# Zeros at the start of a linear-attention and MoE kernel: forty-four products in 64 by 64 tiles, and planned waits near the beginning filled with half the columns

## The chip, the cores and the metric

The kernel runs on one core of one Trainium2 chip. The metric is the time of one execution on the device, in microseconds. Before the change three timed runs gave 536.9, 537.01 and 539.99 us, a median of 537.01 us. One further execution was recorded by the hardware profiler. It took 540.65 us, and 538.9 us lie between its first and its last instruction (the span).

## The reference

A linear attention with a decay for each channel runs over four batches, eight heads and 768 tokens, with heads 48 wide. Its output, 3072 tokens of 384 numbers, goes through two matrix products with a gate between them. All numbers are float32.

```python
for t in range(S):
    kt, vt, rt, wt = (k[:, :, t], v[:, :, t], r[:, :, t], w[:, :, t])
    cur = np.einsum('bhd,bhe->bhde', u[None] * kt, vt)
    y[:, :, t] = np.einsum('bhd,bhde->bhe', rt, state + cur)
    state = wt[:, :, :, None] * state + np.einsum('bhd,bhe->bhde', kt, vt)
...
h = x @ w_in                       # 384 -> 2048
g = np.where(pos, h, np.where(neg, 0.0, (h + beta) ** 2 / (4.0 * beta)))
return (g @ w_out).astype(np.float32)
```

## The kernel before, in words

The tokens are cut into twelve units of 256 (`attention(u, ...)`) and into six blocks of 512 for the two big products (`products(n)`). For each unit the decays `wq` are turned into running products by scans on VectorE (lines 472 and 477), `k` and `r` are scaled with them (498 and 548), and TensorE makes the products among the tokens of a chunk (`among`, line 518), the transposes of `k` (`ktrans`, 557), the state updates (`umat`, 579) and the outputs (627). `among` runs twice for the first three units, the first time on `nk`, which is `k` times `u` from ScalarE (line 488). These attention products are 64 by 64 tiles of float32 in turn on the four quarters of the array; the transposes take 128 by 128.

The sixteen blocks of weights come as raw words (`wraw`, loaded at line 386) and are decoded: ScalarE (398 and 400), GpSimd (402), VectorE (404), ScalarE (394) and VectorE (407). The big products are lines 974 (into `h`) and 994 (into `acc`). `load` (line 333) issues nearly all transfers from SyncE's queue.

The order of all this is not written by hand. `Plan` holds each piece of work as an operation with an engine, an assumed cost, what it reads and writes, and a due time; `best` and `order` make a list for each engine from these. Three things in it concern TensorE alone and compute nothing:

- `warm()` runs `WARM` = 44 products of a tile of zeros (`zero`, set by GpSimd at line 338) with itself, before anything else has to run there. The planner assumes a cost of 5.0 us for them. Each takes the whole array (128 by 128 weights) and 32 columns, through the helper `zeros` (line 357).
- `kept_warm` walks the planned order, and where TensorE is planned to be idle for longer than `IDLE` = 0.6 us, it puts more zeros into a bank that is free at that time, as many columns as fit the gap at `COLUMN` = 0.00168 us each. These are the fills; they too are line 357.
- The gap from time zero to the first operation of TensorE counts as a wait as well: `free` starts at 0.0, and so a fill stands even ahead of the 44 products.

Since all of it is float32, the trace shows two records for one such product, and two weight loads.

TensorE takes its instructions in this fixed order. A zero product that takes longer than planned holds up what is behind it, whether its data are there or not.

Of the kernel before, what the change touches and what calls it, by code (L numbers as in the profile page):

```python
# [42 lines left out]
WARM = 44  # L43

IDLE, COLUMN = 0.6, 0.00168

LANES = 8

# [6 lines left out]
class Plan:  # L55
# [97 lines left out]
    def kept_warm(self, order, engine, banks, fill):  # L153

        ops, begin, end = self.ops, self.begin, self.end
        touched, free, out = {}, 0.0, []
        used = {b: [n for n in order if b in ops[n]["touch"]] for b in banks}
        for n in order:
            op = ops[n]
            if op["e"] == engine:  # L160
                gap = begin[n] - free
                if gap > IDLE:
                    for b in banks:
                        after = next((m for m in used[b] if begin[m] >= begin[n]), None)
                        before = max((end[m] for m in used[b] if begin[m] < begin[n]), default=0.0)
                        if (after is None or ops[after]["fresh"]) and begin[n] - max(before, free) > 0.9 * gap:
                            out.append(lambda b=b, gap=gap: fill(b, gap))
                            break
                free = begin[n] + op["cost"]
            out.append(op["emit"])  # L170
        return out
# [102 lines left out]
def attention_moe(tc, a):  # L274
    nc = tc.nc
    V, A, G, PE = nc.vector, nc.scalar, nc.gpsimd, nc.tensor
# [7 lines left out]
    def tiles(n, shape, dt, name, of=pool):  # L284
        return [of.tile(shape, dt, tag=f"{name}{i}", name=f"{name}{i}") for i in range(n)]

    def one(shape, dt, name, of=pool):
        return tiles(1, shape, dt, name, of)[0]
# [10 lines left out]
    zero = one([128, 128], F32, "zero")  # L299
# [22 lines left out]
    hp = tiles(2, [128, WIDE], F32, "h", psum)  # L322

    bank = [*tiles(3, [128, 512], F32, "bank", psum), *acc, *hp]

    def op(engine, cost, due, reads, writes, emit, **kw):
        return plan.add(engine, cost, emit, due, reads, writes, **kw)
# [8 lines left out]
    SOON = 0, 200.0  # L336
# [15 lines left out]
    def zeros(to, n):  # L352

        while n >= 32:
            m = min(512, n if n < 128 else n // 128 * 128)
            rhs = zero[:, 0:m] if m <= 128 else zero.unsqueeze(1).broadcast_to([128, m // 128, 128])
            PE.matmul(to[:, 0:m], lhsT=zero, rhs=rhs, start=True, stop=True)  # L357
            n -= m

    def warm():  # L360
        for _ in range(WARM):
            zeros(hp[0], 32)

    op("PE", 5.0, SOON, ["zero"], [("b", 6)], warm)


    wraw, w_hi, w_lo = {}, {}, {}
# [472 lines left out]
    for n in range(2 * GUARDED):  # L840
# [10 lines left out]
        out=flag, in0=bank[0][0:1, 0:1], scalar1=127.5, scalar2=None, op0=ALU.is_lt))  # L851

    with tc.manual_schedule(engines=None):
        for emit in plan.kept_warm(plan.best(step_ops, dues), "PE", [("b", i) for i in range(8)],
                                   lambda b, us: zeros(bank[b[1]], int((us - 0.25) / COLUMN))):
            emit()

    for p in (psum, pool):
# [204 lines left out]
```

## Time and profile before

| what | value |
|---|---|
| timed runs, median (lowest to highest) | 537.01 us (536.9 to 539.99) |
| profiled execution | 540.65 us |
| its span | 538.9 us |
| TensorE busy | 524.8 us, 97% |
| VectorE busy | 339.4 us, 63% |
| ScalarE busy | 299.1 us, 56% |
| GpSimd busy | 92.3 us, 17% |
| granted clock, mean | 0.995 |
| moved by DMA | 55.03 MB, mean 102 GB/s |

Time is counted in microseconds from the start of the span. In the rows of the trace the first number is a start, the second a duration; then come engine, line and operation, the tile written, an arrow and the tiles read, and the shapes. In brackets stands how long the engine had been idle, and what ended that. `x88` says that so many records are merged in a row. PE is TensorE's products, PEld its weight loads, DVE is VectorE, ACT ScalarE, POOL GpSimd, and SPq the queue of SyncE that issues transfers. The zeros of the fills and of `warm` count as busy time of TensorE.

### The profile page before, as it was taken

The page shows a single profiled execution, that of the slowest core. Times are in us where ns is not written, and L with a number is a line of the kernel's source. Part 1 is how long each engine was busy: PE and PEld are TensorE (multiplying, and loading weights), DVE is VectorE, ACT ScalarE, POOL GpSimd, SP SyncE. Part 2 cuts the span into 40 slices and gives each one's busy share as a digit, 9 for nine tenths or more (in the row PEclk, how much of TensorE's full clock was granted, in tenths as well). Part 3 has the DMA queues.
Part 4 walks back from the last instruction along what each step waited for, and adds up shares of the span by engine and source line. Part 5 has one row for each costly group of instructions (what it writes and reads, how often), then busy time and mean ns, then how long its engine had stood idle before and what let it go on. Part 6 is the DMA issues. An engine that isn't in the chain of part 4 may idle for free.

```text
span 538.9 us, 13106 instructions
## 1 busy us (share of the span) xinstructions
PE 524.8 (97%) x5556; PEld 438.4 (81%) x5556; DVE 339.4 (63%) x596; ACT 299.1 (56%) x617; POOL 92.3 (17%) x63
## 2 busy tenths in 40 slices
PE   8999989999999999999999999999999999999993
PEld 6977878787899999887878787778877787888882
DVE  5079979998888687744778643887353444333330
ACT  2058869897986556544456354556444434544440
POOL 2053466663120202000102101110000100000000
PEclk9999999999999999999999999999999999999998
DMA  8609481634661515310424301430100100100001
GB/s 323 264 16 338 151 293 77 232 112 137 198 229 52 177 27 202 98 60 2 134 96 137 138 1 48 156 118 6 60 1 0 55 3 13 63 0 0 1 0 66
DMA packets 22067, 55.03 MB, mean 102 GB/s; under 512 B 3120, under 2 KB 8688, under 8 KB 22000
## 3 DMA queue, kind: packets, MB, share of 16 engines
q1 hardware_dynamic: 21856, 53.98, 29.1%
q8 instruction: 45, 0.74, 0.6%
q14 instruction: 22, 0.18, 0.1%
q10 hardware_dynamic: 144, 0.13, 0.1%
HBM read 47.22 MB, written 4.72 MB: 96 GB/s over the span
## 4 chain that ended last, share of the span: by engine, by line
PE 92%; DVE 2%; ACT 1%; SPq 1%; DMA 1%; issue 1%; POOL 0%; DVEq 0%; POOLq 0%
PE h L974 37%; PE acc L994 37%; PE bank L627 4%; PE h L357 3%; PE bank L357 3%; PE bank L579 2%; PE bank L518 2%; PE bank L557 2%; SPq L726 1%; DMA x<-last 1%; DVE fl L404 1%; PE acc L518 0%; DVE r L524 0%; ACT g L789 0%; PE acc L702 0%
## 5 line engine op out<-in xcount | busy, mean ns | idle before, releaser
L974 PE MATMUL h<-x,wt 128*128 128x512 f32 (+1 forms) x1035 | 222.9, 361 | 2.4 <-DMA x<-last 2.1
L974 PEld LDWEIGHTS h<-x,wt 128*128 128x128 f32 x1035 | 170.7, 188 | 33.7 <-DMA x<-last 2.1
L994 PE MATMUL acc<-gh,wt 128*128 128x512 f32 (+1 forms) x690 | 156.4, 362 | 0.0
L791 DVE SCALAR_TENSOR_TENSOR g<-g,h 128x512 f32<-128x512 f32 (+1 forms) x115 | 68.1, 593 | 108.3 <-ACT g L790 106.2
L994 PEld LDWEIGHTS acc<-gh,wt 128*128 128x128 f32 x690 | 115.6, 188 | 21.3
L789 ACT ACTIVATE g<-h 128x512 f32<-128x512 f32 (+1 forms) x115 | 60.6, 527 | 124.1 <-PE h L974 117.2
L794 DVE TENSOR_TENSOR gl<-g,gh 128x512 fp32r<-128x512 f32 (+1 forms) x115 | 71.3, 624 | 28.1 <-ACT gh L793 27.7
L994 PE MATMUL acc<-gl,wt 128*128 128x512 f32 (+1 forms) x345 | 86.3, 358 | 0.0
L793 ACT CAST gh<-g 128x512 fp32r<-128x512 f32 (+1 forms) x115 | 62.5, 546 | 42.4 <-DVE g L791 42.1
L994 PEld LDWEIGHTS acc<-gl,wt 128*128 128x128 f32 x345 | 59.6, 188 | 10.7
L790 ACT ACTIVATE g<-g 128x512 f32<-128x512 f32 (+1 forms) x115 | 64.7, 562 | 3.2
L402 POOL TENSOR_SCALAR wraw<-fl 128x768 uint16<-128x768 f32 x16 | 52.5, 3296 | 64.1 <-ACT wraw L400 64.1
L544 POOL TENSOR_TENSOR r<-cst,d 128x512 f32<-128x512 f32 x18 | 19.7, 1117 | 183.8 <-PE bank L627 168.3
L477 DVE TENSOR_TENSOR_SCAN p<-wq,seeds 128x520 f32<-128x520 f32 x24 | 30.8, 1282 | 3.1 <-DMA wq<-in_w 2.1
L536 POOL TENSOR_TENSOR nk<-nk 128x768 f32<-128x768 f32 x9 | 17.1, 1902 | 81.8 <-DMA nk<-in_nk 81.8
L472 DVE TENSOR_TENSOR_SCAN y<-wq,seeds 128x520 f32<-128x520 f32 x24 | 29.8, 1242 | 0.8
L548 DVE TENSOR_TENSOR rk<-rk,p 128x512 f32<-128x512 f32 x24 | 16.8, 710 | 18.6 <-PE acc L518 18.6
L564 ACT COPY kt<-bank 128x512 f32<-128x512 f32 x24 | 13.5, 582 | 21.3 <-PE bank L557 21.3
L357 PE MATMUL bank<-zero 128*128 128x512 f32 (+12 forms) x64 | 20.8, 457 | 2.3 <-POOL zero L338 2.3
L357 PE MATMUL h<-zero 128*128 128x32 f32 x88 | 19.0, 401 | 0.0
L357 PEld LDWEIGHTS h<-zero 128*128 128x128 f32 x88 | 18.9, 333 | 0.0
L357 PEld LDWEIGHTS bank<-zero 128*128 128x128 f32 x64 | 12.1, 216 | 8.1 <-issue 4.9
(109 smaller groups left out, 434.4 us busy)
## 6 DMA issues: line engine op xcount, KB each, us to landing
rk<-in_rk SPq DMA_DIRECT2D x24, 512.0 KB, 5.2
wraw<-in_wbits SPq DMA_DIRECT2D x16, 768.0 KB, 8.1
nk<-in_nk SPq DMA_DIRECT2D x9, 768.0 KB, 4.7
wq<-in_w SPq DMA_DIRECT2D x24, 260.5 KB, 2.8
vn<-in_v SPq DMA_DIRECT2D x11, 384.0 KB, 6.6
fl<-in_w SPq DMA_DIRECT2D x12, 260.0 KB, 3.8
out_y<-g SPq DMA_DIRECT2D x11, 256.0 KB, 2.4
x<-last SPq DMA_DIRECT2D x66, 32.0 KB, 2.6
```

The costliest lines, as they stand in the source:

```text
L357: PE.matmul(to[:, 0:m], lhsT=zero, rhs=rhs, start=True, stop=True)
L402: op(on, 0.62 if f in SIGNS else 3.2, due, [("fl", k)], [("raw", f)], lambda: e.tensor_scalar(out=half(1), in0=s, scalar1=0.0, scalar2=327 ...
L472: V.tensor_tensor_scan(out=y_[:, ::-1], data0=w[:, SEG:0:-1], data1=sv[:, ::-1], initial=0.0, op0=ALU.mult, op1=ALU.add)
L477: V.tensor_tensor_scan(out=pv[:, q].rearrange("p n c -> p (n c)"), data0=w[:, 0:SEG], data1=sv, initial=0.0, op0=ALU.mult, op1=ALU.add,)
L627: PE.matmul(out=bank[by[g]][HP * half : HP * half + HP, lo : lo + C], start=first, stop=False, skip_group_check=True, **kw)
L789: op("ACT", c, due, [("b", 6 + hk)], [("g", gk)], lambda: nc.scalar.activation(gs, hs, AF.Relu, scale=0.5, bias=0.5))
L790: op("ACT", c, due, (), [("g", gk)], lambda: nc.scalar.activation(gs, gs, AF.Square))
L791: op("DVE", 0.13 + 0.53 * k, due, [("b", 6 + hk)], [("g", gk)], lambda: nc.vector.scalar_tensor_tensor(out=gs, in0=gs, scalar=1.0, in1=hs, ...
L793: op("ACT", c, due, [("g", gk)], [("gh", gk)], lambda: nc.scalar.copy(ghs, gs))
L794: op("DVE", 0.15 + 0.5 * k, due, [("g", gk), ("gh", gk)], [("gl", gk)], lambda: nc.vector.tensor_tensor(out=gls, in0=gs, in1=ghs.bitcast(F ...
L974: nc.tensor.matmul(hp, lhsT=wx[f][:, cs], rhs=xt[:, j, :], start=n == 0, stop=n == 8)
L994: nc.tensor.matmul(o[j], lhsT=wx[f][:, cs], rhs=gt, start=first and i == 0, stop=stop and i == 2, skip_group_check=True)
```

## The change

The 44 products now take a quarter of the array each: 64 rows by 64 columns of `zero` against 32 columns. They go in turn to the four quarters, and the two row halves write to different banks (`hp[0]` and `hp[1]`). Their assumed cost is 3.0 us in place of 5.0. `kept_warm` no longer fills the wait ahead of TensorE's first operation (`and free`), and a fill whose planned start is before `COLD` = 7.0 us gets half the columns.

```diff
+COLD = 7.0
...
-                if gap > IDLE:
+                if gap > IDLE and free:
...
-                            out.append(lambda b=b, gap=gap: fill(b, gap))
+                            out.append(lambda b=b, gap=gap, free=free: fill(b, gap, free))
...
     def warm():
-        for _ in range(WARM):
-            zeros(hp[0], 32)
-
-    op("PE", 5.0, SOON, ["zero"], [("b", 6)], warm)
+        for n in range(WARM):
+            r, c = n % 2 * 64, n // 2 % 2 * 64
+            PE.matmul(hp[n % 2][c : c + 64, 0:32], lhsT=zero[r : r + 64, 0:64], rhs=zero[r : r + 64, 0:32], start=True, stop=True)
+
+    op("PE", 3.0, SOON, ["zero"], [("b", 6), ("b", 7)], warm)
...
-                                   lambda b, us: zeros(bank[b[1]], int((us - 0.25) / COLUMN))):
+                                   lambda b, us, at: zeros(bank[b[1]], int((us - 0.25) / COLUMN / (2 if at < COLD else 1)))):
```

The line numbers of the changed kernel are two or three higher at the places that follow.

On TensorE, this is the start of the program before: a fill of 1190 columns, the 44 products of the whole array (into `h`), a second fill of 240 columns, and then the first work on data, the transposes of `k` and the products of `among`.

```order
L357 MATMUL bank_121<-zero_74 128x512 x2
L357 MATMUL bank_121<-zero_74 128x128
L357 MATMUL bank_121<-zero_74 128x38
L357 MATMUL h_119<-zero_74 128x32 x44
L357 MATMUL bank_121<-zero_74 128x128
L357 MATMUL bank_121<-zero_74 128x112
L557 MATMUL bank_121<-cst_67,rk_81 128x128 x4
L518 MATMUL acc_116<-rk_82,nk_84 64x64
```

After the change the same place begins with the 44 quarter products, of which the last two are shown (the pair stands 22 times); then comes the one fill, and the same work on data.

```order
L365 MATMUL h_119<-zero_74 64x32
L365 MATMUL h_120<-zero_74 64x32
L359 MATMUL bank_121<-zero_74 128x512
L359 MATMUL bank_121<-zero_74 128x384
L359 MATMUL bank_121<-zero_74 128x116
L560 MATMUL bank_121<-cst_67,rk_81 128x128 x4
L521 MATMUL acc_116<-rk_82,nk_84 64x64
```

The first fill is gone, the 44 products stand in its place, and the fill behind them has grown from 240 to 1012 columns, half of what the planned wait there would take: by the rule for a fill's columns, that wait was 0.65 us and is now 3.65 us, 2.0 us of it from the lower assumed cost and 1.0 us from the earlier tile of zeros.

On GpSimd, the start of the program before has the tile `zero` behind two others, `ob` and `g`.

```order
L338 MEMSET seeds_73 128x520
L339 MEMSET seeds_73 128x8
L345 MEMSET ob_112 128x512
L346 MEMSET g_105 128x256
L338 MEMSET zero_74 128x128
L343 MEMSET r_90 128x512
```

After the change the same rows stand in this order.

```order
L340 MEMSET seeds_73 128x520
L341 MEMSET seeds_73 128x8
L340 MEMSET zero_74 128x128
L347 MEMSET ob_112 128x512
L348 MEMSET g_105 128x256
L345 MEMSET r_90 128x512
```

The tile of zeros, which TensorE's first product reads, is set two instructions earlier. Everything else, on all engines and in SyncE's queue, stands in the same order as before up to the end of the program's main part; the later fills are the same too.

## The prediction

> **What bounds the kernel now.** I read the page's chain of work first, the share of the span by engine and by line.
>
> ```profile
> PE 92%; DVE 2%; ACT 1%; SPq 1%; DMA 1%; issue 1%; POOL 0%; DVEq 0%; POOLq 0%
> PE h L974 37%; PE acc L994 37%; PE bank L627 4%; PE h L357 3%; PE bank L357 3%; PE bank L579 2%; PE bank L518 2%; PE bank L557 2%; SPq L726 1%; DMA x<-last 1%; DVE fl L404 1%; PE acc L518 0%; DVE r L524 0%; ACT g L789 0%; PE acc L702 0%
> ```
>
> TensorE sets the end, and line 357, the zeros, holds 6% of the span on that chain although it computes nothing. The same chain in order of time shows where.
>
> ```profile
> 2.35 4.49 PE bank L357 x8
> 6.84 18.76 PE h L357 x88
> 27.44 1.74 PE acc L518 x64
> ```
>
> The first fill takes 4.49 us, the 44 products 18.76 us (planned: 5.0), and the first products on data begin only at 27.4 us. Were the data late too, that would cost nothing. So I asked the timeline what the other engines did.
>
> ```profile
> 7.74 0.69 DVE L498 TENSOR_TENSOR rk<-rk,y 128x512 f32<-128x512 f32 x1
> 8.51 0.91 ACT L488 ACTIVATE nk<-rk,cst 128x256 f32<-128x256 f32 x2 [0.49 <-DMA rk<-in_rk]
> 9.92 0.69 DVE L498 TENSOR_TENSOR rk<-rk,y 128x512 f32<-128x512 f32 x1
> 27.37 1.81 PE L518 MATMUL acc<-rk,nk 64*64 64x64 f32 x64
> 27.48 0.59 ACT L564 COPY kt<-bank 128x512 f32<-128x512 f32 x1 [18.05 <-PE bank L557]
> 29.25 1.30 DVE L548 TENSOR_TENSOR rk<-rk,p 128x512 f32<-128x512 f32 x2 [18.64 <-PE acc L518]
> 30.28 0.94 ACT L398 ACTIVATE fl<-wraw 128x768 f32<-128x768 f32 x1
> ```
>
> The last input of the first products (line 518) is `nk`, ready at 8.51 + 0.91 = 9.42 us. `rk` is complete at 9.92 + 0.69 = 10.61 us. From then on ScalarE and VectorE stand for 18 us, and both waits end on TensorE. The transfers stand as well: here are the first 60 us in 40 slices, busy tenths of the DMA engines and GB/s.
>
> ```profile
> DMA  0799999999999980000000000049999989930000
> GB/s 0 208 382 282 379 414 438 418 388 422 392 391 389 410 355 4 0 0 0 0 0 11 0 0 0 11 139 372 361 399 401 316 286 357 403 122 25 5 0 0
> ```
>
> They are full to about 22 us and then empty to about 39 us. So until 27 us the kernel is bound by its own zeros. After that VectorE has no gaps to speak of: in these two stages, behind the length come the busy times of TensorE, of its weight loads and of VectorE, the last of them 9.31 of 10 and 19.06 of 20 us.
>
> ```profile
> 30.00:40.00 10.00, 9.97 (x265) 7.94 (x264) 9.31 (x16) 6.97 (x11) 7.55 (x3) 1.00 0.04 11
> 40.00:60.00 20.00, 19.43 (x313) 15.13 (x312) 19.06 (x31) 16.41 (x36) 10.60 (x4) 1.00 0.64 235
> ```
>
> **The change: when TensorE comes free.** First its clock, since it prices the zeros. The granted clock in the rows is 1.00 from the start, but the weight loads tell another story (duration least, median, most).
>
> ```profile
> L357 PEld LDWEIGHTS h<-zero x88: 333/333/333, 6.6 to 25.1; 128*128 128x128 f32 x88
> L518 PEld LDWEIGHTS acc<-rk,nk x64: 135/223/228, 27.4 to 28.9; 64*64 64x64 f32 x64
> L518 PEld LDWEIGHTS bank<-rk,nk x128: 129/135/135, 45.9 to 69.9; 64*64 64x64 f32 x128
> L994 PEld LDWEIGHTS acc<-gh,wt 128*128 128x128 f32 x690 | 115.6, 188 | 21.3
> ```
>
> A 128 by 128 load takes 333 ns in each of the 88 zero records, and 188 ns in the big products; a 64 by 64 load falls from 223 to 135 ns within the first call of line 518. So the array ran slowly until nearly 28.9 us, all zeros included.
>
> *Start.* The zeros wait for their tile on GpSimd.
>
> ```profile
> 1.38 0.53 POOL L345 MEMSET ob<- 128x512 f32 x1
> 2.09 0.20 POOL L338 MEMSET zero<- 128x128 f32 x1
> ```
>
> Moved ahead of `ob` and `g`, the tile starts at about 1.38, is set at 1.58, and TensorE starts 0.06 later as now (2.29 to 2.35): at 1.64 us. The other two come 0.2 us later, long before their use.
>
> *The 44 products.* Nothing in the trace runs 32 columns on a quarter of the array. The nearest row is line 518, the same quarter tiles in the same alternation with 64 columns: 64 records in 1.74 us slow, which is 27 ns each. At that, 88 records take 2.4 us. Below, 64 records in 1.16 us fast (the row of line 518 at 49.80, further down) give 18 ns, 1.6 us in all; above, 213 ns as now, 18.8 us, if the quarters did not overlap. I take 2.4, whose row is much the nearer: zeros done at 4.0 us.
>
> *The fill.* 4.49 us for 1190 columns is 3.77 ns a column slow; 1012 columns take 3.8 us, and end at 7.9 us. Fast, these rows give 1.84 us for 970 columns (512 + 384 + 74, by the program's order), 1.90 ns, and 1.9 us.
>
> ```profile
> 26.38 1.06 PE L557 MATMUL bank<-cst,rk 128*128 128x128 f32 x4
> 29.11 0.65 PE L557 MATMUL bank<-cst,rk 128*128 128x128 f32 x4
> 34.05 1.84 PE L357 MATMUL bank<-zero 128*128 128x512 f32 x6
> 49.80 1.16 PE L518 MATMUL bank<-rk 64*64 64x64 f32 x64 [0.35 <-DVE rk L548]
> ```
>
> *The first work on data.* The transposes (line 557) need `k`, ready at 7.74 + 0.69 = 8.43 us, later than the fill's end. They end at 9.1 (0.65 us, fast) or 9.5 (1.06, slow), and line 518 needs `nk` at 9.42. So it starts at about 9.5 us either way, where it now starts at 27.37: **17.9 us earlier**, and set by data in place of zeros. The two edits overlap there: of the 25.05 us between 2.35 and 27.4 some 1 us turns into waiting for data.
>
> *The clock at that point.* In the new order TensorE is busy from 1.64 to 7.9 us and again from 8.43 us. If the clock has risen by 9.5 us, line 518 takes 1.16 us in place of 1.81, 0.65 us more, and VectorE's line 548 starts at 10.7 (its own previous work ends at 10.61) in place of 29.25: **18.5 us earlier**. If not, 17.9. I take 18.5.
>
> The Trainium skill's page "TensorE: Matmul & The Clock Gate" (Part 1) says that the array starts at half its clock and gets the whole once a free-running window of about 3.4 us has been busy. The trace agrees with such a window only if it has to be busy throughout: 4.49 us of unbroken zeros did not raise the clock for the 88 records behind them. By a plain 3.4 us of activity the estimate for line 518 would be the fast 1.16 us, and the total 18.5; by what the trace did after 2.35 us it could be 17.9.
>
> **What is late next.** All else keeps its order, so what follows moves by 18.5 us, unless a transfer is not there. SyncE's early issues do not wait for TensorE, so their landings stay.
>
> ```profile
> 4.53 1.16 SPq L386 DMA_DIRECT2D wraw<-in_wbits  x2
> DMA to landing us min/median/max: 7.2/7.8/8.4
> 6.84 0.44 SPq L386 DMA_DIRECT2D wraw<-in_wbits  x1
> DMA to landing us min/median/max: 9.5/9.5/9.5
> 14.57 0.43 SPq L386 DMA_DIRECT2D wraw<-in_wbits  x1
> DMA to landing us min/median/max: 8.8/8.8/8.8
> 32.20 0.90 ACT L398 ACTIVATE fl<-wraw 128x768 f32<-128x768 f32 x1
> 32.45 9.03 POOL L402 TENSOR_SCALAR wraw<-fl 128x768 uint16<-128x768 f32 x3 [28.82 <-ACT wraw L400]
> 34.07 0.90 ACT L398 ACTIVATE fl<-wraw 128x768 f32<-128x768 f32 x1
> 38.71 0.33 SPq L333 DMA_DIRECT2D wq<-in_w  x1
> 40.05 0.91 SPq L386 DMA_DIRECT2D wraw<-in_wbits  x2
> 50.22 0.93 ACT L398 ACTIVATE fl<-wraw 128x768 f32<-128x768 f32 x1
> ```
>
> The raw words of the first three blocks land at 11.7, 13.5 (5.1 + 8.4) and 16.3 us. Their decodes on ScalarE, now at 30.28, 32.20 and 34.07, would stand at 11.8, 13.7 and 15.6: the first two just fit, the third is 0.7 us late. Behind it waits GpSimd's line 402, but that takes three blocks in a row at 3 us each from 32.45 and reaches the third at 38.5, some 2 us after its words are there, so I cost it at nothing; without that cover it would be 0.7 us. The next transfer, at 38.71, would be issued at 20.2, when the fourth block is still landing (14.57 + 8.8 = 23.4). Up to 3 us of backlog replace an empty queue. The words issued behind it, at 40.05, are decoded at 50.22, ten microseconds later, so this too costs nothing; without that margin it costs up to 3 us.
>
> *The sum.* 540.65 (the profiled execution; 538.9 of span and 1.75 around it) less 18.5 gives 522.1 us; I say **522**. The profiled execution is 3.6 us over the median of the timed runs, 537.01, while one timed run, 539.99, is near it. There are two readings. Either some executions run part of the zeros at the raised clock: at double rate, about 3.6 us of that stretch would give 3.6 us. Then that difference goes with the zeros, and all executions come to 522. Or recording costs 3.6 us, and timed runs come to 537.0 - 18.5 = 518.5. Since a timed run shows the longer time as well, the first is a little likelier.
>
> **The rivals.**
>
> *The clock stays low longer.* The wait before 8.43 us and the one before 9.5 break the busy stretch, and if no window is full by then, the products behind run slowly too: the second transposes 0.41 us more (1.06 against 0.65), the second call of line 518 0.58 (1.74 against 1.16), line 579, with as many records as line 518 and 1.15 us fast, about 0.5.
>
> ```profile
> 87.20 1.15 PE L579 MATMUL bank<-vn,kt 64*64 64x48 f32 x64
> ```
>
> From 17.9 that leaves 16.4 us, or 524 us. For it speaks that 25 us of zeros did not raise the clock; against it, that about 6 us are now unbroken, and it rose within 2.5 us of the transposes at 26.38.
>
> *Loads become the bound.* The decodes have margins of 0.1 and 0.2 us, and the queue is full until 23 us. If they land later than before or the backlog is not covered, 2 to 3 us are lost: 524 to 525 us. Against it speaks that no early issue is moved.
>
> *The quarters do not overlap* and each record takes 213 ns still: zeros to 20.4, fill to 24.2, transposes to 25.3 against 27.4. That is a gain of 2 us, 538 us, no change. Line 518's 27 ns speak against it.
>
> *Slower, by the clock.* If the long stretch of zeros was what let the clock rise soon after it, and the new start leaves the array slow through the VectorE-bound stage, where it is fed in short pieces, TensorE's work doubles there: it is busy 19.43 us of the stage from 40 to 60. The point from which this decides is 18.5 us of such work on the path, so the clock would have to stay low to about what is now 50 us; low through 60 us it is some 30 us more, 552 us. The unchanged fills of that stage, which kept it up before, speak against it.
>
> **How the numbers follow.** The forecast gets 0.72 (522 with 0.45, 518.5 with 0.27), the clock rival 0.10, the loads 0.08, tiles that do not overlap or overlap in part 0.07, the slow array 0.03. A range from 517.5 to 525.5 us holds the first three, with half a microsecond to a microsecond at each end for the sizes; 0.10 lies outside. About 1%, 5.4 us, is what a measurement of this kernel can tell from no change. Faster by more: 0.94 (the first three and tiles that overlap in part); within: 0.04; slower: 0.02, the rest of the slow array's chance falling within 1%.
>
> **What would show it.** Right: the 44 products in under 3 us with 64 by 64 weight loads; line 518 starting near 9.5 us behind `nk` and not behind zeros; VectorE's 18.64 us wait at line 548 gone; no empty stretch of the DMA queues between 22 and 39 us; every later row about 18 us earlier. Wrong: weight loads of line 518 still at 223 ns beyond the second call (the clock), ScalarE's line 398 waiting for `wraw` (the loads), or a shift that shrinks again between 10 and 60 us. That the pace of the rest depends on something other than its order, such as a transfer that now meets another, is what would make me wrong without any of these.

## The result, and the profile after

The changed kernel takes 522.24 us (median of four runs, 521.2 to 523.71), the kernel before 536.95 us in the same comparison: a ratio of 0.9713, with a 95% interval from 0.967 to 0.9757. The recorded execution took 523.71 us with a span of 521.9 us, 16.9 and 17.0 us less than that of before.

First the chain of work of the changed kernel, by engine and by line, as the page gives it.

```profile
PE 92%; DVE 2%; DMA 2%; ACT 1%; SPq 1%; issue 1%; DVEq 0%; ACTq 0%
PE h L977 38%; PE acc L997 38%; PE bank L630 5%; PE bank L359 2%; PE bank L582 2%; PE bank L521 2%; PE bank L560 2%; DMA cst<-in_consts 1%; DMA x<-last 1%; SPq L729 1%; PE acc L630 0%; DVE fl L407 0%; DVE rk L551 0%; SPq L335 0%; ACT g L792 0%
```

The 44 products (`h` at line 365 now) are gone from it, and at its beginning stands a transfer, the load of `cst`: the start is bound by data. The fills that are left are the later ones. The timeline of the changed kernel, at the places that were shown of before:

```profile
1.38 0.20 POOL L340 MEMSET zero<- 128x128 f32 x1
1.64 2.57 PE L365 MATMUL h<-zero 64*64 64x32 f32 x88 [1.64 <-POOL zero L340]
4.14 3.76 PE L359 MATMUL bank<-zero 128*128 128x512 f32 x6
8.33 0.91 ACT L491 ACTIVATE nk<-rk,cst 128x256 f32<-128x256 f32 x2 [0.23 <-DMA rk<-in_rk]
8.57 0.66 PE L560 MATMUL bank<-cst,rk 128*128 128x128 f32 x4 [0.67 <-DVE rk L501]
9.15 1.16 PE L521 MATMUL acc<-rk,nk 64*64 64x64 f32 x64
10.61 1.29 DVE L551 TENSOR_TENSOR rk<-rk,p 128x512 f32<-128x512 f32 x2
14.53 0.93 ACT L401 ACTIVATE fl<-wraw 128x768 f32<-128x768 f32 x1 [0.58 <-DMA wraw<-in_wbits]
17.24 0.93 ACT L401 ACTIVATE fl<-wraw 128x768 f32<-128x768 f32 x1 [0.68 <-DMA wraw<-in_wbits]
14.04 8.89 POOL L405 TENSOR_SCALAR wraw<-fl 128x768 uint16<-128x768 f32 x3 [10.40 <-ACT wraw L403]
```

TensorE now waits for VectorE ahead of the transposes, and VectorE's line 551 follows at 10.61 us without a wait, where the same instruction stood at 29.25. The weight loads of the zeros and of line 521's first call (least, median, most, in ns):

```profile
L365 PEld LDWEIGHTS h<-zero x88: 177/223/223, 1.6 to 3.8; 64*64 64x64 f32 x88
L521 PEld LDWEIGHTS acc<-rk,nk x64: 129/135/135, 9.2 to 10.0; 64*64 64x64 f32 x64
```

The zeros ran slowly, and the first products on data at the full rate. The DMA engines have lost about half of their empty stretch (first 60 us, 40 slices).

```profile
DMA  0799999999999997999999950000028999736999
GB/s 0 202 371 278 381 419 414 449 367 418 403 386 386 412 366 231 368 412 395 418 344 422 414 209 8 5 0 0 11 49 303 365 316 387 275 75 186 366 356 373
```

They are now full to about 35 us in place of 22, and an empty stretch from 36 to 44 us is left of the one from 22 to 39. One thing on TensorE is new, and VectorE waits for it.

```profile
14.57 0.25 PE L582 MATMUL bank<-g,kt 64*64 64x48 f32 x1 [1.47 <-issue]
14.96 0.36 DVE L598 TENSOR_TENSOR ob<-h,ptot 128x192 f32<-128x192 f32 x1 [1.79 <-PE h L582]
```

In the middle of line 582 TensorE stands for 1.47 us and waits for nothing that the profile shows ("issue"). In the kernel before that VectorE instruction was this row:

```profile
31.72 0.35 DVE L595 TENSOR_TENSOR ob<-h,ptot 128x192 f32<-128x192 f32 x1
```

So the lead over before is 29.25 - 10.61 = 18.6 us at line 551 and 31.72 - 14.96 = 16.8 us four VectorE instructions later. It stays close to that: the last long piece of the chain, 36 records of line 994 (997 after), starts at 521.57 and at 504.58 us.

```profile
521.57 8.44 PE acc L994 x36
504.58 8.44 PE acc L997 x36
```

### The profile page after: what moved, and what is told of

It reads as the page before. It is cut to its first block, busy times and chain, and to the rows that moved or that the text cites. A ratio compares the mean times of both kernels' runs of the same rounds, so it can differ in the third digit from the quotient of the medians.

```text
span 521.9 us, 13096 instructions
## 1 busy us (share of the span) xinstructions
PE 506.1 (97%) x5550; PEld 419.8 (80%) x5550; DVE 340.8 (65%) x596; ACT 299.5 (57%) x617; POOL 93.1 (18%) x63
## 4 chain that ended last, share of the span: by engine, by line
PE 92%; DVE 2%; DMA 2%; ACT 1%; SPq 1%; issue 1%; DVEq 0%; ACTq 0%
PE h L977 38%; PE acc L997 38%; PE bank L630 5%; PE bank L359 2%; PE bank L582 2%; PE bank L521 2%; PE bank L560 2%; DMA cst<-in_consts 1%; DMA x<-last 1%; SPq L729 1%; PE acc L630 0%; DVE fl L407 0%; DVE rk L551 0%; SPq L335 0%; ACT g L792 0%
## 5 line engine op out<-in xcount | busy, mean ns | idle before, releaser
L797 DVE TENSOR_TENSOR gl<-g,gh 128x512 fp32r<-128x512 f32 (+1 forms) x115 | 73.3, 641 | 28.3 <-ACT gh L796 27.8
L359 PE MATMUL bank<-zero 128*128 128x512 f32 (+11 forms) x58 | 18.9, 454 | 0.0
L403 ACT ACTIVATE wraw<-wraw 128x768 uint16<-128x768 uint32 x16 | 17.3, 1083 | 0.3
L501 DVE TENSOR_TENSOR rk<-rk,y 128x512 f32<-128x512 f32 x24 | 17.0, 709 | 0.7 <-DMA rk<-in_rk 0.4
L630 PEld LDWEIGHTS bank<-rk,st 64*64 64x64 f32 x656 | 12.3, 134 | 6.3 <-issue 4.4
L527 DVE COPY_PREDICATED r<-below,bank 128x512 f32<-128x512 int32 x22 | 15.1, 728 | 3.1 <-PE bank L521 3.1
L407 DVE SCALAR_TENSOR_TENSOR fl<-fl,wraw 128x768 int32<-128x768 int32 x16 | 16.8, 1056 | 0.0
```

The lines of the kernel that those rows point to most:

```text
L630: PE.matmul(out=bank[by[g]][HP * half : HP * half + HP, lo : lo + C], start=first, stop=False, skip_group_check=True, **kw)
L797: op("DVE", 0.15 + 0.5 * k, due, [("g", gk), ("gh", gk)], [("gl", gk)], lambda: nc.vector.tensor_tensor(out=gls, in0=gs, in1=ghs.bitcast(F ...
```

## Experiments

Three questions were open. Which edit brings the gain? What is the gap of 1.47 us? And why did the recorded executions move by 16.9 us and the timed ones by 14.7? Theory F for the gap: TensorE had run out of fetched instructions, whose next block stood behind the loads in the DMA queues. Rival G: line 582 waits for something of its own. Records are counted here as products and weight loads of TensorE from the start of the trace, in order; in the changed kernel the gap begins at record 444.

**The tiles alone.** Only `warm` is changed. The cost of 5.0 us stays, a fill still stands ahead of the 44 products, and no fill is halved. The tile of zeros is set earlier here too, and by the rule for a fill's columns the first fill shrinks from 1190 to 595 columns and the second grows from 240 to 835, so the edit is not quite the tiles alone.

```diff
-        for _ in range(WARM):
-            zeros(hp[0], 32)
-    op("PE", 5.0, SOON, ["zero"], [("b", 6)], warm)
+        for n in range(WARM):
+            r, c = n % 2 * 64, n // 2 % 2 * 64
+            PE.matmul(hp[n % 2][c : c + 64, 0:32], lhsT=zero[r : r + 64, 0:64], rhs=zero[r : r + 64, 0:32], start=True, stop=True)
+    op("PE", 5.0, SOON, ["zero"], [("b", 6), ("b", 7)], warm)
```

> The 44 products run in quarter tiles, but the fill ahead of them stays and no fill is halved, and the cost stays at 5.0 us: a fill of 595 columns, the 44 products, a fill of some 830 columns. Theory (the length of the zeros on TensorE ahead of the first data sets the start, and the 44 whole-array products at 213 ns a record were nearly all of it): TensorE starts at 1.64 us, then 2.2 us of fill, 2.6 of products and 2 to 3 of fill end between 8.6 and 9.6 us, where data come at 8.5; so line 518's first call starts at 9.2 to 10.2 us and the time is that of the change or up to 1 us more, 522 to 523 us. Rival (the missing first fill and the halved columns are what brings the gain): most of the gain is lost, over 530 us.

Measured: 524.69 us median (521.3 to 526.29), a ratio of 0.9732 to the kernel before, interval 0.9672 to 0.9791. In its trace the zeros end before the data, and line 519, the first call of `among`, starts at 9.84 us, as expected. The time is above the expected 522 to 523 us. The gap is there too, at record 444.

```profile
9.26 0.66 PE L558 MATMUL bank<-cst,rk 128*128 128x128 f32 x4 [1.51 <-DVE rk L499]
9.84 1.16 PE L519 MATMUL acc<-rk,nk 64*64 64x64 f32 x64
15.29 0.25 PE L580 MATMUL h<-g,kt 64*64 64x48 f32 x1 [1.51 <-issue]
```

This edit brings 12.3 us of the 14.7 that the whole change brought. The recorded execution, 526.29 us, lost more after the gap: its clock fell for one stretch. The stages below end with three numbers, the clock, the DMA share and GB/s.

```profile
5.40:15.60 10.20, 6.71 (x194) 4.96 (x194) 7.40 (x11) 6.11 (x12) 0.87 (x1) 1.00 1.03 400
15.60:19.00 3.40, 3.40 (x78) 3.14 (x70) 1.66 (x4) 2.69 (x3) 3.40 (x2) 0.50 1.04 400
```

**The fills alone.** As the changed kernel, with the 44 products over the whole array.

```diff
-        for n in range(WARM):
-            r, c = n % 2 * 64, n // 2 % 2 * 64
-            PE.matmul(hp[n % 2][c : c + 64, 0:32], lhsT=zero[r : r + 64, 0:64], rhs=zero[r : r + 64, 0:32], start=True, stop=True)
+        for _ in range(WARM):
+            zeros(hp[0], 32)
```

> As the changed kernel, but the 44 products take the whole array again. Theory: 1.64 + 18.8 us of products + 3.8 of fill + 1.06 of transposes put line 518's first call at 25.3 us, 2 us before where it is in the kernel before: 534 to 538 us. Rival (the fills bring the gain): under 530 us.

Measured: 536.05 us median (534.91 to 537.87), ratio 0.9973, interval 0.9948 to 0.9998.

```profile
1.64 18.98 PE L359 MATMUL h<-zero 128*128 128x32 f32 x88 [1.64 <-POOL zero L340]
20.43 3.74 PE L359 MATMUL bank<-zero 128*128 128x512 f32 x6
24.95 1.64 PE L520 MATMUL acc<-rk,nk 64*64 64x64 f32 x64
```

The first data products start at 24.95 us, close to the 25.3 that was expected, and 2.4 us earlier than in the recording of before. By the medians the fills and the earlier tile of zeros are worth 0.9 us, which counts as no change here (most timed executions of the kernel before run part of their zeros at the raised clock, as a later experiment shows).

**No products of zeros.** The 44 are left out, the fill of 1012 columns stays.

```diff
-WARM = 44
+WARM = 0
```

> As the changed kernel, but without the 44 products; the fill of 1012 columns stays. Two theories of the 1.5 us in which TensorE stood in the middle of line 579 (582 in the changed kernel) from 13.1 to 14.57 us though no wait is written there. F: its next instructions had not been fetched; it runs out after some 444 records of products and weight loads, and the fetch stands behind the loads. G: the wait belongs to line 582 itself, its operands or its bank. Without 176 of these records F expects no gap in line 582, and any gap some 176 records later. G expects the same 1.5 us there. Clock: the fill ends at 5.4 us, so unless it has risen by then, line 518's first call takes 1.8 us and the next ones are slow too, 0.7 to 2 us more. F gives 520.5 to 523, G 522.5 to 524.5.

Measured: 524.86 us median (522.47 to 529.47), ratio 0.9741, interval 0.9686 to 0.9796. The gap in the first call of line 582 is gone, as F has it (one of 1.38 us stands at record 1207, from 39.9 us on), but the time is above the range that F was given.

```profile
9.58 1.11 PE L560 MATMUL bank<-cst,rk 128*128 128x128 f32 x4 [4.18 <-DVE rk L501]
10.62 1.99 PE L521 MATMUL acc<-rk,nk 64*64 64x64 f32 x64
8.80:15.50 6.70, 5.92 (x98) 4.40 (x102) 5.29 (x8) 3.56 (x8) 0.00 (x0) 0.50 1.02 412
```

The clock, which rose once near 5.4 us, was low again from 8.8 to 15.5 us, after TensorE had waited 4.18 us. The first products took 1.99 us in place of 1.16. So in this execution the lack of zeros cost what they are for, the raised clock at the first work on data.

**Two long products in place of 44 short ones.**

```diff
-        for n in range(WARM):
-            r, c = n % 2 * 64, n // 2 % 2 * 64
-            PE.matmul(hp[n % 2][c : c + 64, 0:32], lhsT=zero[r : r + 64, 0:64], rhs=zero[r : r + 64, 0:32], start=True, stop=True)
+        for h, n in ((hp[0], 512), (hp[1], 128)):
+            zeros(h, n)
```

> As the changed kernel, but in place of the 44 quarter products two of the whole array, of 512 and 128 columns, which take the same 2.4 to 2.6 us with 8 records in place of 176 of each two kinds. The array is as busy as before, so the clock rises by 9.2 us as in the changed kernel. F (instructions not fetched): no gap in line 582, 1.0 to 1.7 us less than the changed kernel, about 520.7. G (the wait belongs to line 582): the gap stays, 522.2.

Measured: 524.31 us median (523.92 to 526.35), ratio 0.9743, interval 0.9694 to 0.9793. Line 582 runs through, but the time did not fall, so half of this expectation failed.

```profile
18.05 0.91 PE L359 MATMUL bank<-zero 128*128 128x512 f32 x2 [1.73 <-issue]
40.18 0.32 PE L581 MATMUL bank<-vn,kt 64*64 64x48 f32 x6 [1.09 <-issue]
```

The gap has moved some 3 us on, into a fill: it starts at record 443 again. A shorter one of 0.65 us follows at record 698 and one of 1.09 us at record 1207, about 255 and three times 255 further. G is out, since line 582 has nothing to do with it; the count is what stays. Taking records away from the front does not remove the gap but puts it at another instruction, since the next block is asked for later as well.

**Twice as many.**

```diff
-WARM = 44
+WARM = 88
```

> As the changed kernel, but 88 quarter products in place of 44, so 176 more records of products and weight loads ahead of the data, and 2.1 to 2.6 us more of zeros. F (TensorE runs out of fetched instructions after some 444 records): the gap without a written wait starts at record 443 or 444 again, which now lies in the first call of line 518 (521 in the changed kernel), at 10 to 11 us, and not in line 582. G (the wait belongs to line 582): it is in line 582 again. Time 522 to 526 us.

Measured: 525.12 us in one execution. Neither expectation held: no gap at record 444, and one of 2.23 us at record 700, 256 further on, in the second call of line 521. (The time lay within the 522 to 526 us that were expected. After the gap the clock was low from 16.97 to 20.38 us.)

```profile
16.90 0.33 PE L521 MATMUL h<-rk 64*64 64x64 f32 x1 [2.23 <-issue]
```

For F that says that here the first block was in time, and the next was not. The queue that carries instructions (q8 in the table of DMA queues) shows when: its first transfer of 16 KB started at 6.99 us here, and at 11.99 us in the changed kernel, where it ended at 12.95, 1.6 us ahead of the end of the gap. The same holds wherever TensorE stood so: all nine gaps of 0.65 us and more end 1.3 to 1.6 us after the first, second or fourth transfer of this queue has ended, at records 444, 700 and 1207 in turn. So F's condition is when a block is asked for, not how many records there are.

**The kernel before, twice more, and the changed kernel again.** These ask about the third question. C: some executions run part of the zeros at the raised clock. R: recording costs 2 to 4 us.

> The kernel before, unchanged, recorded once more. Its timed runs lie from 535.8 to 540.5 us and its first recorded execution took 540.65. C (some executions run part of the zeros at the raised clock): where this execution comes out near 537 us, its 88 zero records take some 3.4 us less than 18.76, with weight loads below 333 ns in part of them; where it is near 540, they take 18.76 again. R (recording costs 2 to 4 us): it takes 539 to 541 us, and the zeros 18.76 us.

> The kernel before a third time, for the same question: C expects the 88 records' time to follow the execution's time one for one, R expects neither to move.

> The changed kernel, unchanged, recorded once more. Line 518's first call (521) again starts when the data come, at 9.1 to 10.3 us, whether the clock has risen or not, and the gap without a written wait is at record 443 or 444 again (F). R expects 523 to 524.5 us for the recorded execution, 1.5 us over the timed ones; if recording costs nothing, 521 to 523.

Measured: 536.31, 538.44 and 521.87 us, one execution each. All three lie among the timed ones, so R is not borne out here. It isn't excluded as a part either: in seven of the eight comparisons with several runs of the kernel in question, the recorded execution was the longest, by 1.5 to 5 us against the median of the others. In the second recording of before the chain and the zeros' weight loads read:

```profile
2.35 3.85 PE bank L357 x8
6.20 16.26 PE h L357 x88
L357 PEld LDWEIGHTS h<-zero x88: 192/333/333, 6.0 to 22.0; 128*128 128x128 f32 x88
5.40:8.80 3.40, 3.40 (x30) 3.13 (x30) 3.26 (x6) 1.70 (x6) 0.00 (x0) 1.00 1.04 382
8.80:25.80 17.00, 17.00 (x133) 16.67 (x135) 1.66 (x2) 1.05 (x3) 0.00 (x0) 0.50 0.82 324
```

The clock was up for one stretch of 3.4 us and down again under the short zeros, and fill and zeros took 20.1 us in place of 23.25. In the third they took 20.1 us as well, with 15.85 us for the 88 records. So C holds in part: some executions of the kernel before run part of the zeros at the raised clock, and the recording that the prediction used was one without any. That the whole time follows the zeros one for one failed: the third execution had zeros as short as the second and took 2.1 us more. The timed executions agree with this. Of 22 of the kernel before in two comparisons, six have a mean clock of 0.994 to 0.996, like the first recording, and a median of 539.6 us; sixteen have 0.976 to 0.981, like the other two, and a median of 537.3. (The mean reads lower in the faster ones because a low clock shows in it only once the clock has changed.) The changed kernel repeats itself, gap included:

```profile
14.41 0.25 PE L582 MATMUL bank<-g,kt 64*64 64x48 f32 x1 [1.47 <-issue]
```

**A few products more, to ask for the block earlier.** If F is right, the changed kernel has just too few records (188) ahead of its first wait for data.

```diff
-WARM = 44
+WARM = 52
```

> The changed kernel with 52 quarter products in place of 44: 32 more records, 220 in place of 188 ahead of the first instruction that waits for data. F: the second block of instructions is asked for when TensorE's queue has taken in some 200 records. With 188 that happens only when the wait for the data is over at 8.4 us, and the block is there at 14.4; with 220 it happens before that wait, so the block comes some 4 us earlier and the gap at record 444 is gone. Zeros end at about 8.3 us, still before the data. Then 1.5 us less than the changed kernel: 520.5 us. If the gap only moves one block on (record 700), or if F is wrong about what sets the request: 522 to 523 us.

> The same with 60 products, 252 records. F: no gap at record 444 either. Zeros end at 8.6 to 8.8 us if the clock has not risen, 0.2 us after the data: 520.5 to 521 us; 522 to 523.5 if a gap at record 700 takes its place.

> The changed kernel itself on the same chip, to compare the two with: 521 to 523 us, the gap at record 443 or 444.

Measured in one comparison: 521.32 us with 52 (520.85 to 522.71, ratio to before 0.9675, interval 0.9648 to 0.9701), 521.79 us with 60 (520.9 to 522.47, ratio 0.9687, 0.9659 to 0.9714), and 523.89 us for the changed kernel (522.35 to 525.71, ratio 0.9721, 0.9692 to 0.9751). All three lie 0.8 us or more above what was expected of them (520.5, 520.5 to 521, and 521 to 523). The timeline with 52:

```profile
1.64 3.00 PE L365 MATMUL h<-zero 64*64 64x32 f32 x104 [1.64 <-POOL zero L340]
9.82 1.33 PE L521 MATMUL acc<-rk,nk 64*64 64x64 f32 x64 [0.70 <-ACT nk L491]
13.68 0.34 DVE L598 TENSOR_TENSOR ob<-h,ptot 128x192 f32<-128x192 f32 x1
14.74 0.73 DVE L527 COPY_PREDICATED r<-below,acc 128x512 f32<-128x512 int32 x1 [0.71 <-DMA below<-in_below]
```

Line 598 no longer waits and stands at 13.68 us in place of 14.96, although the data came 0.6 us later in this execution. No gap is left at record 444 or 700, with 52 or with 60. VectorE's next instruction now waits 0.71 us for a load, that of `below`. In the kernel before and in the changed one the same instruction had these rows:

```profile
32.58 0.74 DVE L524 COPY_PREDICATED r<-below,acc 128x512 f32<-128x512 int32 x1 [0.52 <-PE h L518]
15.92 0.73 DVE L527 COPY_PREDICATED r<-below,acc 128x512 f32<-128x512 int32 x1 [0.60 <-PE acc L521]
```

So without the gap it stands 1.2 us earlier, and a load bounds it there. The transfers of the 1.1 us from 6.9 us on show the block (first line), and in the changed kernel it stands in the 1.1 us from 11.9 us on, by the same line of the table (second).

```profile
q8 instruction: 1, 0.02, 5.1%
q8 instruction: 1, 0.02, 5.5%
```

With eight products of zeros more, the median is 2.6 us lower in this comparison. The gap accounts for about 1.2 us of that in the traces. The intervals of 52 and 44 still overlap at the edge, those of 52 and 60 for the most part, and the recorded execution of the changed kernel, 525.71 us, also had its clock low from 57.8 to 61.2 us, after a wait for data, which the ones with 52 and 60 had not. So that the gap is gone is shown; how much time that saves is not settled.

What was not tried apart is F's second half, that the loads in the DMA queues are what delays a block.

## Why the prediction was right, and where it was not

- **The bound before** was read rightly. The tiles, with little else changed, bring 12.3 of the 14.7 us, the fills without the tiles 0.9, and the other engines' 18 us waits are gone.
- **Start and zeros.** 1.64 us was forecast and measured. The 44 products took 2.57 us against 2.4, the fill 3.76 against 3.8. The rival of tiles that do not overlap is out. The row of line 518, a product with twice the columns, was 7% low. The clock had risen during that row; a call of it that ran slow throughout, in the kernel without the 44, took 1.99 us for 64 records, 31 ns each, against 29 ns for the zeros. So at the low clock the quarter products hardly got cheaper with their columns.
- **The first data.** Line 518 (521) was forecast at 9.5 us, behind `nk`, and stands at 9.15, straight behind the transposes and with no wait for `nk` in its row (with 52 products it did wait for `nk`, 0.70 us); VectorE's line 548 (551) was forecast 18.5 us earlier and is 18.6 us earlier.
- **The clock** had risen in time: after 6.3 us of unbroken zeros the transposes at 8.57 us took 0.66 us, the fast time. Once it has changed, the clock stays at one value for 3.4, 6.8, 10.2 or 17.1 us between changes in the first 27 us of these executions, multiples of 3.4. The page "TensorE: Matmul & The Clock Gate" (Part 1) of the Trainium skill speaks of a free-running window of about 3.4 us, and these stretches agree with it. The rival of a clock that stays low was real but took place in other kernels: without the 44 products, and for one stretch of 3.4 us after the gap with the tiles alone (1.51 us) and with 88 products (2.23 us). In three recordings of the changed kernel the gap of 1.47 to 1.49 us did not lower it.
- **The loads** cost nothing through the weights, as forecast. The second and third blocks were 0.6 and 0.7 us late on ScalarE, where the second had been forecast to just fit, and GpSimd's three decodes still ran without a pause, 8.89 us from 14.04. The backlog after 20 us cost nothing that shows.
- **The step that failed** is "all else keeps its order, so what follows moves by 18.5 us, unless a transfer is not there". I listed the data that TensorE needs, and left out its instructions. In the three recordings of the kernel before, with its slow zeros, no such gap stands in the first 60 us, so the blocks of instructions came in time; now 1.47 us of TensorE, 1.8 us of VectorE, go to waiting for one. At the first use of `below` the lead is down to 32.58 - 15.92 = 16.7 us. Without the gap, with 52 products, it is 32.58 - 14.74 = 17.8 us, and there the load of `below` bounds it. "Their landings stay" failed by this much: that load landed at about 13.8 us before and at 14.6 to 14.7 us after, with 44 products and with 52, and I had not listed it. So of the 1.9 us by which the lead fell, about 1.2 are the late instructions; the rest would have gone to the load. That is why the recorded executions differ by 16.9 us and not by 18.5.
- **The total** came out at 522 in part by luck, from two errors that offset each other. The sum started from a recorded execution, and against the recorded one of the changed kernel, 523.71, it is 1.6 us low; the median of the four runs lies 1.5 us below that execution. Executions of the changed kernel differ by about as much among themselves. The second recording, 521.87, had the same gap and was still 1.8 us shorter; 1.2 us of that are the small transfers of line 729 at 52.7 us, which took 3.81 us in the first recording and 2.60 in the second, by the chain of each:

```profile
52.73 3.81 DMA x<-last
52.71 2.60 DMA x<-last
```

  Of the two readings of the difference between recorded and timed executions, the likelier one held in the main: a large part went with the zeros, and timed executions gained 14.7 us, not 18.5. That recording adds some of it is not excluded.

## What to carry to other kernels

Price filler work by its rows in the trace, not by its planned cost: products meant to take 5 us took 18.8 and held up an engine whose data had been there for 18 us. When an engine's wait goes, ask for everything that it consumes next, its instructions as well as its data; here, pauses that were put down to "issue" at a fixed count of instructions were late blocks of instructions, and the DMA table's row of the instruction queue showed it. Eight more products of filler had the block transferred 5 us earlier, and the pause went. And compare several executions of each kernel before an offset of 2 us is explained: the same program differed by as much.

## What the runs showed of the hardware that was not expected

- TensorE's gaps without a shown wait began at records 443 or 444 in five recorded executions of three kernels, at 698 or 700 in two and at 1207 in two: about 255 or a multiple of that apart. Each ended 1.3 to 1.6 us after a transfer of 16 KB in the instruction queue had ended. In the changed kernel, with the DMA queues full, it took 6 us from the end of the wait for data (8.57 us) to the end of the gap (14.57). With 52, 60 and 88 products the first block was transferred from 6.8 to 7.0 us on, with 44 (188 records ahead of the wait for data) from 12.0 to 12.4, and with the tiles alone (196 records) from 12.8. So the request seems to come with a record between 196 and 220; that is inferred from where it happened and was not tried apart.
- Short zeros over the whole array, 32 columns each, did not hold the clock: in the second recording of the kernel before it fell from 1.00 to 0.50 after 2.6 us of them (6.20 to 8.82 us), with TensorE's busy share at 100% in that stage.
- The clock in the rows is 1.00 until the first change that the profile has. The first recording of the kernel before shows 1.00 with weight loads of 333 ns, the later one 0.50 with the same 333 ns. The duration of weight loads tells the clock where that row can't.
